# First loads, first scores and gradient sums reordered in a decode attention-and-MLP kernel with its backward pass

## The chip, the cores and the metric

The kernel runs on one core of one Trainium2 chip. The metric is the device time of one execution in microseconds (us). All timed runs quoted here are in the fast state, except e5, a single run whose state is unknown, and "time" is the median of an experiment's runs. The engines are PE (TensorE), DVE (VectorE), ACT (ScalarE), POOL (GpSimd) and SP (SyncE, which here issues the loads). "Head" is one of the 32 attention heads.

## The reference, cut to what matters

The forward pass is a gated sum of single-query attention over a cache and a small MLP; the backward pass returns gradients of all inputs.

```python
q = (x @ wq).reshape(B, Sq, H, Dh)             # x: 1x640, wq: 640x4096, 32 heads of 128
scores = einsum("bhqd,bhkd->bhqk", q, k_cache) * Dh**-0.5    # k_cache: 32 x 4096 x 128
o = einsum("bhqk,bhkd->bhqd", softmax(scores), v_cache)
a = o.reshape(B, Sq, H*Dh) @ wo                # wo: 4096x640
g = sigmoid((x * gate_w).sum(-1)); out = g*a + (1-g)*mlp(B_x)
# out, and by jax.vjp: dx, dK, dV (each 32 MB), dwq, dwo, dw1, db1, dw2, dgate_w
```

K and V are read once (2 MB per head) and dK and dV are written once (2 MB per head). With the weights and their gradients that makes 82 MB in and 82 MB out.

## The kernel before

Loads go out through SP in program order. Stores go out through GpSimd (all but the last small ones). Four K and four V buffers let the loads run ahead: K of head h+3 is issued in head h, and it needs the buffer of head h-1. The start:

```python
nc.scalar.dma_start(vec_rows[0:RC, :], x_rows)              # three first vectors, 5 rows of 256 B each, by ACT
nc.scalar.dma_start(vec_rows[RC:2 * RC, :], dy_rows)
nc.scalar.dma_start(vec_rows[2 * RC:3 * RC, :], gw_rows)
...
load_wq(0); load_wo(0); load_k(0); load_v(0); load_k(1); load_v(1); load_wo(1)    # on SP, one call per line
...  # w1, b1
load_k(2); load_v(2); load_w2(0); load_w2(1)                # w2: 96 partitions, rows of 7680 B
...  # K3 and V3 follow in head 0
```

The vectors give the gate, the gate gives the output gradient `da_bc`, and from `da_bc` and wo come four sums on DVE ("output-gradient sums"), which are broadcast as a row (`dbc`) and turned into columns (`dcol`). Small work like this sits in a list of steps. A `slot` takes from it what is ready, at most `p` PE steps and `d` DVE steps:

```python
prep_steps(0, 0)                       # qcol, doa, dob (the sums), qbc, dbc (row), dcol, qdc (columns)
for _ in range(8):
    slot(0, 9, 9)                      # all of it, ahead of head 0's scores
tk = []
for c in range(NT):
    k_chunk(0, c, tk)                  # transposes of K on PE, copied out by ACT
    if c: s_chunk(0, c - 1, tk)        # scores
...
for h in range(H):
    hh, g = h % G, h // G              # groups of four heads
    if hh == 3:
        load_wo(g + 2)                 # waits until the gradient dwo, made in the same buffer, is stored
        if g % 2 == 0:
            load_wq(g // 2 + 1)        # needs the buffer that the dx sums read
    load_k(h + 3); load_v(h + 3)
    if hh == 1 and g + 1 < NG:         # steps of the next group go to the head of the list
        rest = steps[:]; steps.clear(); prep_steps(g + 1, h); steps.extend(rest)
    period(h)                          # softmax, dV, dK, ... with three slots in it
```

## Time and profile before

| | before |
|---|---|
| time, median of 3 runs | 417.72 us (417.38 to 417.74) |
| bytes moved | 165.06 MB |
| busiest compute engine | PE and DVE, 74% each |
| DMA rate where it is full | about 420 GB/s |

165.06 MB at 422 GB/s are 391 us by themselves. These are lines of the page of the kernel before. The second is the busy share of the DMA engines in 40 equal slices, in tenths; the third is the rate in the same slices; the last is the chain of waits, by engine:

```profile
span 415.7 us, 15639 instructions
...
DMA  8999999999999999999999999999999999998980
GB/s 280 419 401 335 420 424 417 420 423 423 421 423 420 420 404 415 424 420 423 423 410 426 423 414 411 419 422 381 405 411 423 419 419 422 421 422 351 401 314 14
...
DMA 37%; DVE 30%; PE 21%; ACT 6%; issue 2%; ACTq 0%; DVEq 0%
```

The start, from the timeline of the kernel before (start, duration, engine, line, operation, count, and in brackets the idle time before and what ended it):

```profile
7.05 0.17 PE L174 MATMUL cols_ps<-ident_bf,vec_rows 15*128 15x15 bf16 x1 [7.05 <-DMA vec_rows<-in_gate_w_dram]
...
11.55 0.83 DVE L268 SCALAR_TENSOR_TENSOR junk<-wo_g,da_bc 128x640 bf16<-128x640 bf16 x1 [1.14 <-ACT da_bc L214]
...
15.25 0.61 PE L103 MATMUL d_ps<-ident_bf,do4b 128*128 128x128 bf16 x4 [2.15 <-DVE do4b L272]
...
16.66 1.87 PE L535 MATMUL tr<-ident_bf,Kn 128*128 128x128 bf16 x16
...
21.61 0.19 DVE L605 TENSOR_REDUCE m<-sA 128x1 f32<-128x32 f32 x1 [4.61 <-PE sA L543]
...
28.97 0.67 POOL L584 DMA_DIRECT2D out_dram<-dV_sb  x1 [27.58 <-DVE o_all L646]
```

PE has nothing to do until it uses the vectors at 7.05. The transposes of K stand behind the row of the output gradient (15.25) in PE's order. Head 0 proper begins with the maximum of its scores, `m`, at 21.61, and its first store is issued at 28.97.

In the middle, from the waits view of the kernel before, cut to 260 to 285 us (total, times, longest):

```profile
PE qc_ps L258 <- DMA wq_g<-in_A_wq_dram: 11.8, 1, 11.8
```

PE stands still for 11.8 us for a wq load. In this stretch the DMA runs at 424 GB/s, so by itself the wait costs nothing.

### The profile page before, as it was taken

To read this page: it belongs to the slowest core of one execution; us is meant where nothing else is said; L and a number is where in the kernel's file an instruction comes from. 1 tells how busy PE (TensorE), PEld (TensorE's weight loads), DVE (VectorE), ACT (ScalarE), POOL (GpSimd) and SP (SyncE) were. 2 spreads that over 40 slices of the span, in tenths; PEclk is the share of its full clock that TensorE was granted. 3 is DMA by queue.
4 is the path that set the end of the run, shared out by engine and by line. 5 is a ranking of instruction groups with operands and counts; after the bars stand their busy time and mean duration, and the time that the engine had idled before them with its cause. 6 is when DMAs were issued, how large, how long until landed. Compare 5 with 4: busy or idle time off the path is not lost.

```text
span 415.7 us, 15639 instructions
## 1 busy us (share of the span) xinstructions
PE 305.6 (74%) x6932; PEld 281.1 (68%) x6932; DVE 308.2 (74%) x804; ACT 174.4 (42%) x394; POOL 49.3 (12%) x92
## 2 busy tenths in 40 slices
PE   0787999888998788788877688429888788876200
PEld 0676888888987677787767687428777678876200
DVE  2348666665679999989897688528999997967850
ACT  1354444334445455354533346305553545553000
POOL 0001110111110111121111112001111111132310
PEclk9999999969999999989996899958999999998655
DMA  8999999999999999999999999999999999998980
GB/s 280 419 401 335 420 424 417 420 423 423 421 423 420 420 404 415 424 420 423 423 410 426 423 414 411 419 422 381 405 411 423 419 419 422 421 422 351 401 314 14
DMA packets 26336, 165.06 MB, mean 397 GB/s; under 512 B 2812, under 2 KB 2812, under 8 KB 10012
## 3 DMA queue, kind: packets, MB, share of 16 engines
q1 hardware_dynamic: 14116, 82.03, 48.6%
q0 software_dynamic: 12112, 82.03, 47.7%
q8 instruction: 54, 0.88, 0.8%
q14 instruction: 14, 0.11, 0.1%
q10 hardware_dynamic: 40, 0.01, 0.0%
HBM read 82.03 MB, written 82.03 MB: 395 GB/s over the span
## 4 chain that ended last, share of the span: by engine, by line
DMA 37%; DVE 30%; PE 21%; ACT 6%; issue 2%; ACTq 0%; DVEq 0%
DMA Kn<-in_A_k_cache_dram 30%; PE tr L535 7%; DVE dK_sb L557 7%; DVE dV_sb L557 6%; DMA out_dram<-dK_sb 6%; ACT tT L537 5%; DVE junk L354 4%; PE sA L601 3%; PE sA L543 3%; PE sB L654 3%; DVE junk L268 3%; PE h_ps L385 2%; DVE junk L486 2%; DMA vec_rows<-in_gate_w_dram 1%; DVE wo_g L343 1%
## 5 line engine op out<-in xcount | busy, mean ns | idle before, releaser
L537 ACT COPY tT<-tr 128x512 f32<-128x512 f32 x256 | 142.9, 587 | 153.1 <-PE tr L535 153.0
L543 PEld LDWEIGHTS <-tT 128*128 128x128 bf16 x2048 | 75.8, 98 | 37.0 <-ACT tT L537 31.6
L535 PE MATMUL tr<-ident_bf,Kn 128*128 128x128 bf16 x1024 | 79.2, 230 | 9.4 <-DMA Kn<-in_A_k_cache_dram 8.2
L557 DVE TENSOR_TENSOR dV_sb<-p_bf,qd 128x2048 bf16<-128x2048 bf16 x64 | 78.0, 1218 | 4.1 <-DMA out_dram<-dK_sb 4.1
L557 DVE TENSOR_TENSOR dK_sb<-ds_bf,qd 128x2048 bf16<-128x2048 bf16 x64 | 77.7, 1216 | 0.0
L535 PEld LDWEIGHTS <-Kn 128*128 128x128 bf16 x1024 | 66.2, 104 | 10.9 <-DMA Kn<-in_A_k_cache_dram 9.3
L535 PE MATMUL tr<-ident_bf,Vn 128*128 128x128 bf16 x1024 | 72.8, 221 | 0.2 <-DMA Vn<-in_A_v_cache_dram 0.2
L543 PE MATMUL sA<-qdc,tT 128*128 128x48 bf16 x1024 | 49.2, 188 | 23.0 <-ACT dq_all L659 16.3
L535 PEld LDWEIGHTS <-Vn 128*128 128x128 bf16 x1024 | 63.2, 100 | 1.4 <-issue 0.7
L543 PE MATMUL sB<-qdc,tT 128*128 128x48 bf16 x1024 | 46.3, 183 | 0.6 <-issue 0.6
L654 PE MATMUL sB<-ds_bf,Kn 128*128 128x48 bf16 x1024 | 32.6, 185 | 7.7 <-DVE ds_bf L643 4.8
L584 POOL DMA_DIRECT2D out_dram<-dV_sb x32 | 18.3, 571 | 169.1 <-DVE dV_sb L557 82.1
L601 PEld LDWEIGHTS <-Vn 128*128 128x128 bf16 x1024 | 30.3, 96 | 10.4 <-issue 10.3
L601 PE MATMUL sA<-e_bf,Vn 128*128 128x48 bf16 x1024 | 30.9, 183 | 7.4 <-DVE zs L621 5.4
L574 POOL DMA_DIRECT2D out_dram<-dK_sb x31 | 17.7, 570 | 153.1 <-DVE rz L623 84.6
L654 PEld LDWEIGHTS <-Kn 128*128 128x128 bf16 x1024 | 29.7, 97 | 8.3 <-issue 8.3
L605 DVE TENSOR_REDUCE m<-sA 128x1 f32<-128x32 f32 x32 | 6.1, 189 | 31.7 <-PE sA L543 31.5
L268 DVE SCALAR_TENSOR_TENSOR junk<-wo_g,da_bc 128x640 bf16<-128x640 bf16 x32 | 26.3, 821 | 2.9 <-DMA wo_g<-in_A_wo_dram 1.2
L354 DVE SCALAR_TENSOR_TENSOR junk<-wq_g,dq_bc 128x1024 bf16<-128x1024 bf16 (+1 forms) x25 | 25.1, 1004 | 0.2
L385 PE MATMUL h_ps<-cols_bf,w_sb 128*96 128x1 bf16 x90 | 18.3, 314 | 1.2 <-ACT qd L279 0.5
L641 DVE TENSOR_SCALAR_CACHE_REDUCE dj<-sB,rz 128x128 f32<-128x128 f32 x32 | 11.1, 345 | 10.8 <-PE sB L635 10.8
L385 PEld LDWEIGHTS <-w_sb 128*96 128x96 bf16 x90 | 17.6, 272 | 1.6 <-issue 0.6
(137 smaller groups left out, 277.5 us busy)
## 6 DMA issues: line engine op xcount, KB each, us to landing
Kn<-in_A_k_cache_dram SPq DMA_DIRECT2D x32, 1024.0 KB, 27.0
Vn<-in_A_v_cache_dram SPq DMA_DIRECT2D x32, 1024.0 KB, 27.8
out_dram<-dV_sb POOLq DMA_DIRECT2D x32, 1024.0 KB, 12.3
out_dram<-dK_sb POOLq DMA_DIRECT2D x31, 1024.0 KB, 12.4
wq_g<-in_A_wq_dram SPq DMA_DIRECT2D x4, 1280.0 KB, 21.8
wo_g<-in_A_wo_dram SPq DMA_DIRECT2D x8, 640.0 KB, 13.3
out_dram<-wo_g POOLq DMA_DIRECT2D x8, 640.0 KB, 11.3
out_dram<-dwq_t POOLq DMA_DIRECT2D x5, 896.0 KB, 16.2
```

Of the source, the lines that this page charges most:

```text
L268: nc.vector.scalar_tensor_tensor(junk[:, 0:D], in0=wos[g][:, i, :], scalar=1.0, in1=da_bc[:], op0=ALU.mult, op1=ALU.mult, accum_out=gp["do ...
L354: nc.vector.scalar_tensor_tensor(junk[:, c0:c1], in0=wqs[w][:, rc, c0:c1], scalar=1.0, in1=dq_bc[:, w * WG * Dh + c0:w * WG * Dh + c1], op ...
L385: nc.tensor.matmul(hps[a][:, fc:fc + 1], lhsT=w1_sb[:, rc, :].rearrange("p (q c) -> p q c", c=FCN)[:, :, fc], rhs=x_bf[:, rc:rc + 1], star ...
L535: nc.tensor.transpose(tp[:, t, :], src[:, c * 8 + t, :], ident_bf[:])
L537: nc.scalar.copy(f32v(sb[:].rearrange("p a b -> p (a b)")), f32v(tp[:].rearrange("p a b -> p (a b)")))
L543: nc.tensor.matmul(out[:, j:j + W], lhsT=tb[:, t, :], rhs=vec.to_broadcast([P, W]), start=True, stop=True)
L557: nc.vector.tensor_tensor(dst[:, a:b, :].rearrange("p j (a b) -> p j a b", b=2), col[:, a:b, :].unsqueeze(2).to_broadcast([P, n, Dh // 2, 2]),
L574: nc.gpsimd.dma_start(dKv[h], st["dK"][:])
L584: nc.gpsimd.dma_start(dVv[h], st["dV"][:])
L601: nc.tensor.matmul(O, lhsT=vts[h][:, j, :], rhs=st["e"][:, j:j + 1].to_broadcast([P, W]), start=(j == 0), stop=(j == J - 1))
L641: nc.vector.tensor_scalar(dj[:], PT, rz[:], None, ALU.mult, ALU.add, accum_out=dd[:])
L654: nc.tensor.matmul(DQ, lhsT=kts[h][:, j, :], rhs=ds[:, j, 0:1].to_broadcast([P, W]), start=(j == 0), stop=(j == J - 1))
```

## The change

The intent is to start head 0 earlier (vectors by GpSimd, K second, scores ahead of the columns) and to take the wq wait away (dwo and the dx sums, which release the wo and wq buffers, ahead of the next group's preparation; wq loaded one head earlier). Cut to its core:

```diff
-    nc.scalar.dma_start(vec_rows[0:RC, :], x_rows)            # and the two others
+    nc.gpsimd.dma_start(vec_rows[0:RC, :], x_rows)
 ...
     load_wq(0)
+    load_k(0)
     load_wo(0)
-    load_k(0)
 ...  # qdc split: qs scales the q columns early, qdc the output-gradient columns later
-        add(n("dwo"), "D", dwo, (n("aadd"),))                 # and the dx sums
+        add(n("dwo"), "D", dwo, (n("aadd"),), first=True)
 ...
-    for _ in range(8):
-        slot(0, 9, 9)
+    for _ in range(3):
+        slot(0, 1, 9)
 ...  # K transposes and scores of head 0
+    while steps:
+        slot(0, 9, 9)
 ...
+        if hh == 2 and g % 2 == 0:
+            load_wq(g // 2 + 1)                               # ahead of load_k(h + 3)
         if hh == 3:
             load_wo(g + 2)
-            if g % 2 == 0:
-                load_wq(g // 2 + 1)
 ...
-            rest = steps[:]
-            steps.clear()
+            ahead = [st for st in steps if st[5]]             # steps marked first stay in front
+            rest = [st for st in steps if not st[5]]
+            steps[:] = ahead
             prep_steps(g + 1, h)
```

More of the change, by code (lines that the diff above doesn't have):

```diff
@@ L107 @@
     vec_rows = const.tile([3 * RC, P], BF16, name="vec_rows")
-    nc.scalar.dma_start(vec_rows[0:RC, :], x_rows)
-    nc.scalar.dma_start(vec_rows[RC:2 * RC, :], dy_rows)
-    nc.scalar.dma_start(vec_rows[2 * RC:3 * RC, :], gw_rows)
+    nc.gpsimd.dma_start(vec_rows[0:RC, :], x_rows)
+    nc.gpsimd.dma_start(vec_rows[RC:2 * RC, :], dy_rows)
+    nc.gpsimd.dma_start(vec_rows[2 * RC:3 * RC, :], gw_rows)
     kts, vts, wqs, wos = {}, {}, {}, {}
@@ L227, with add @@
     steps, done = [], {}
-    def add(name, kind, fn, deps=(), head=0):
-        steps.append((name, kind, fn, tuple(deps), head))
+    def add(name, kind, fn, deps=(), head=0, first=False):
+        steps.append((name, kind, fn, tuple(deps), head, first))
     slot_no = [0]
@@ L239, in slot @@
             for st in list(steps):
-                name, k, fn, deps, head = st
+                name, k, fn, deps, head, _ = st
                 if k != kind or head > h or not room[k]:
@@ L292, in qdc, with qs @@
         def qdc():
-            gp["qdc"] = small.tile([P, 2, G], BF16, name="qdc", tag="qdc")
-            nc.vector.tensor_scalar(gp["qdc"][:, 0, :], gp["qc"][:], scale, None, ALU.mult)
-            nc.vector.tensor_scalar(gp["qdc"][:, 1, :], gp["dc"][:], scale, None, ALU.mult)
+            nc.vector.tensor_scalar(gp["dcs"][:], gp["dc"][:], scale, None, ALU.mult)
+        def qs():
+            gp["qcs"] = small.tile([P, G], BF16, name="qcs", tag="qcs")
+            gp["dcs"] = small.tile([P, G], BF16, name="dcs", tag="dcs")
+            nc.vector.tensor_scalar(gp["qcs"][:], gp["qc"][:], scale, None, ALU.mult)
         n = lambda x: f"{x}{g}"
         add(n("qcol"), "P", qcol, (), head)
+        add(n("qs"), "T", qs, (n("qcol"),), head)
         add(n("doa"), "D", do_part(0, 2), (), head)
@@ L370, in finish_steps @@
             elif g % 2 == 1:
-                add(n(f"dx{rc}_"), "D", dx(rc, 0, WG * Dh, g // 2), (n("dqb"),))
+                add(n(f"dx{rc}_"), "D", dx(rc, 0, WG * Dh, g // 2), (n("dqb"),), first=True)
     def mlp_steps():
@@ L551, in s_chunk @@
             sts[h] = {"A": sa_ps.tile([P, 512], F32, name="sA", tag="sA")}
-        products(sts[h]["A"][:, 0:J + W], ts[c], c, gp["qdc"][:, 0, h % G:h % G + 1])
+        products(sts[h]["A"][:, 0:J + W], ts[c], c, gp["qcs"][:, h % G:h % G + 1])
     def outer(dst, col, row, half):
@@ L593, in period @@
         DP, DQ, PT = B[:, 0:J + W], B[:, 128:128 + W], B[:, 256:384]
-        vec = gp["qdc"][:, 1, h % G:h % G + 1]
+        vec = gp["dcs"][:, h % G:h % G + 1]
         tv, tk = [], []
@@ L690 @@
         hh, g = h % G, h // G
+        if hh == 2 and g % 2 == 0:
+            assert g == 0 or f"dx{RC - 1}_{g - 1}" in done
+            load_wq(g // 2 + 1)
         if hh == 3:
@@ L693 @@
             load_wo(g + 2)
-            if g % 2 == 0:
-                assert g == 0 or f"dx{RC - 1}_{g - 1}" in done
-                load_wq(g // 2 + 1)
         load_k(h + 3)
```

## The prediction

> **What bounds it now.** The DMA engines. The page's slice line shows them at 9 tenths in nearly every slice, at about 420 GB/s; 165.06 MB at 422 GB/s alone is 391 us of the 415.7 us span. No compute engine is over 74% busy. 30% of the chain of waits is K loads, among them four waits of 25 to 35 us: they queue on a full DMA (the windows view shows 423 GB/s from 265 to 278 us, while PE stands still). Only DMA time that is idle or slow can be won. From the windows, in full-rate terms:
> - 0 to 7 us: start and the wq load at about 300 GB/s (3.5 us);
> - 30 to 35 us: 243 GB/s (2 us). These are w2 loads, whose 7680-byte packets take about 530 ns, a K packet 315; the first store, issued at 28.97, shows its first packet only at 34.9;
> - 245 to 255 and 280 to 300 us: about 2 us;
> - 375 to 380 us: 295 GB/s (1.5 us); then some 10 us of drain.
>
> **What the change does.** No byte goes away; it reorders.
> 1. Vectors by GpSimd. By ACT the third lands at 6.91 us (issue 1.63, 5.28 to landing), behind the 2 KB packets of wq. By GpSimd I expect 4 to 6.5 us. The Trainium skill, "DMA: Bandwidth & Descriptors", "Issuing engines are not separate DMA queues", says that all issuers share the 16 engines: no bandwidth is gained, only a place in line. If the first store's 5.9 us is a first-use cost, the vectors land no earlier, but the first store does.
> 2. K before wo. wo lands about 2.5 us later (an estimate: 1 MB at 420 GB/s), near 11 us. The output-gradient sums began at 11.55, bound by the gate chain, and become bound by wo. Steps 1 and 2 together win 0.5 to 1 us.
> 3. Scores ahead. The three slots before the scores still hold the broadcast of the output-gradient row, so K's transposes (16.66) still wait on PE for its sums (15.1). Only the columns (0.27 us on PE, plus waiting for ACT) leave the path: 0.7 us. Head 0 starts 1 to 2.5 us earlier in all, and stores begin that much earlier, beside the slow w2 loads: 0.5 to 1.5 us of DMA time.
> 4. dx and dwo ahead of the next group's sums, wq one head earlier. DVE work is the same. The dwo store goes out 3 to 5 us earlier, and SP, which waits 60 us in 5 pieces for wo's buffer (once 18 us, 225.8 to 244.4, followed by the standstill), waits less. PE's standstill may shrink by 5 us, but DMA is full there: only the dips of 245 to 300 us come back, 0.5 to 1 us.
>
> **Time.** Gains of 1 to 3.5 us, and up to 1 us lost elsewhere: 415.2 us, 80% range 412.5 to 418. 3% faster (below 409.4), 95% within, 2% slower (above 426.1).
>
> **What would show it.** Head 0's maximum of the scores at 19 to 20.5 us instead of 21.6; the last vector before 6.5; the first store issued before 28; SP's wait for wo's buffer below 45 us; the same MB and about 420 GB/s between 40 and 370; the last K load issued 1 to 4 us before 345.9.
>
> **What would make it wrong.** Vectors later than 7 us; wq, now ahead of K, holding SP until the dx sums are done, so that stores run dry; another pattern of standstills; a longer drain on the engines that finish last (26 GB/s from 404 to 411 us).

## The result, and the profile after

Ratios are the mean time of one kernel's fast runs over the mean of the other's in the same rounds, so not quite the ratio of the medians.

| | before | after |
|---|---|---|
| median | 417.73 us | 419.11 us (418.71 to 419.51) |
| ratio | | 1.0033, 95% interval 1.0016 to 1.0051 |

The change makes the kernel slower by a third of a per cent. The prediction had it faster by 2.5 us. Page of the changed kernel:

```profile
span 417.1 us, 15646 instructions
...
GB/s 277 420 402 324 421 418 419 423 423 423 420 423 420 420 420 420 422 420 422 422 416 425 419 418 425 421 353 335 395 408 423 423 423 423 421 422 390 407 311 14
...
DVE 33%; DMA 32%; PE 22%; ACT 6%; issue 4%; POOL 0%; ACTq 0%; DVEq 0%; POOLq 0%
```

The fourth slice is slower than before (324 against 335), and so are those from 270 us on (353, 335). Three slices are better by over 10 GB/s (the 15th, the 25th and the 37th). The start, from its timeline:

```profile
2.44 0.52 POOL L110 DMA_DIRECT2D vec_rows<-in_gate_w_dram  x1
...
9.10 0.17 PE L174 MATMUL cols_ps<-ident_bf,vec_rows 15*128 15x15 bf16 x1 [9.10 <-DMA vec_rows<-in_gate_w_dram]
...
17.30 0.61 PE L103 MATMUL d_ps<-ident_bf,do4b 128*128 128x128 bf16 x4 [2.15 <-DVE do4b L272]
...
17.70 1.91 PE L539 MATMUL tr<-ident_bf,Kn 128*128 128x128 bf16 x16
...
22.37 0.18 DVE L609 TENSOR_REDUCE m<-sA 128x1 f32<-128x32 f32 x1
...
29.66 0.58 POOL L588 DMA_DIRECT2D out_dram<-dV_sb  x1 [26.03 <-DVE o_all L650]
```

The vectors are used at 9.10 instead of 7.05, and everything behind them is 2.05 us late (the row of the output gradient: 17.30 instead of 15.25). The new order takes 1.3 us of that back: the maximum comes at 22.37, only 0.76 us late.

The waits of the changed kernel, cut to 250 to 275 us:

```profile
PE tr L539 <- DMA Kn<-in_A_k_cache_dram: 13.8, 1, 13.8
```

The wait for wq is gone, and a wait for K of 13.8 us has come in its place. SP's issues show why, first before and then after:

```profile
225.41 0.33 SPq L117 DMA_DIRECT2D Kn<-in_A_k_cache_dram  x1
225.80 0.47 SPq L122 DMA_DIRECT2D Vn<-in_A_v_cache_dram  x1
244.43 0.33 SPq L132 DMA_DIRECT2D wo_g<-in_A_wo_dram  x1
244.85 0.43 SPq L127 DMA_DIRECT2D wq_g<-in_A_wq_dram  x1
...
260.66 6.98 SPq L122 DMA_DIRECT2D Vn<-in_A_v_cache_dram  x1
```

```profile
221.56 0.38 SPq L127 DMA_DIRECT2D wq_g<-in_A_wq_dram  x1
225.53 7.19 SPq L117 DMA_DIRECT2D Kn<-in_A_k_cache_dram  x1
232.76 4.66 SPq L122 DMA_DIRECT2D Vn<-in_A_v_cache_dram  x1
245.38 0.33 SPq L132 DMA_DIRECT2D wo_g<-in_A_wo_dram  x1
...
251.90 3.09 SPq L122 DMA_DIRECT2D Vn<-in_A_v_cache_dram  x1
273.79 0.33 SPq L117 DMA_DIRECT2D Kn<-in_A_k_cache_dram  x1
```

The K load is issued at the same time in both (225.4 and 225.5), but in the changed kernel it stands behind 1.3 MB of wq. It is used at 268.8, 43 us later. The head that waits for it makes no stores: GpSimd issues none from 259.3 to 278.5. That alone need not cost anything. In the kernel before GpSimd issues none from 263.7 to 280.3, and the DMA stays at 424 GB/s until 280, with SP issuing loads until 267.6. In the changed kernel SP issues nothing from 255.0 to 273.8, so that loads and stores run short together:

```profile
270.00:275.00 5.00, 4.47 (x94) 4.06 (x92) 0.33 (x2) 3.25 (x6) 0.00 (x0) 0.74 0.79 308
275.00:280.00 5.00, 4.68 (x121) 4.32 (x121) 4.05 (x9) 3.46 (x7) 0.54 (x1) 1.00 0.96 395
280.00:285.00 5.00, 4.76 (x135) 4.47 (x130) 4.93 (x15) 2.21 (x6) 0.53 (x1) 1.00 0.77 298
```

These are windows of the changed kernel. Their last three columns are the granted clock, the DMA share and GB/s. The same windows of the kernel before:

```profile
270.00:275.00 5.00, 0.00 (x0) 0.00 (x0) 0.00 (x0) 0.00 (x0) 0.00 (x0) 0.50 1.01 424
275.00:280.00 5.00, 2.46 (x50) 2.18 (x51) 1.81 (x5) 0.16 (x1) 0.00 (x0) 0.50 1.01 424
280.00:285.00 5.00, 4.47 (x90) 4.27 (x88) 4.06 (x13) 2.68 (x6) 1.06 (x2) 0.72 0.95 363
```

**Where the time goes.** Both kernels move the same bytes, so I added up the trace's DMA packet records: how many bytes have landed by a given moment, and how far a kernel is behind the kernel before, in us at 420 GB/s (an own sum, from one profile each; negative is ahead):

```
                                    by 24 us  40 us   260 us  300 us  370 us  400 us
after                                 0.13    0.30   -0.49    2.53    2.47    1.09
e1  before, vectors by GpSimd         0.01    0.87    1.04    2.51    2.35    1.86
e2  before, new start order           0.01   -0.67   -0.91   -0.61   -0.59   -0.41
e4  before, new dx/dwo/wq order       0.03    0.35   -0.39    1.41    1.60    0.55
e8  two slots                        -0.08   -1.60   -1.79   -1.71   -1.74   -1.94
e9  two slots, K first                0.04   -2.12   -1.79   -1.22   -1.28   -0.73
e10 two slots, new dx/dwo/wq          0.07   -1.44   -2.12    0.14    0.28   -0.88
e11 e10 with wq behind K and V       -0.01   -2.42   -2.82   -1.95   -2.15   -2.41
e13 after, vectors by ACT             0.03   -1.09   -1.44    0.50    0.88   -0.46
e16 e11, vectors first on SP          1.01   -0.01   -0.64    0.53    0.40    0.11
```

Differences of a few tenths say little: e3 and e4 begin as the kernel before does, and are at -0.25 and 0.35 by 40 us. There are two places where kernels part: 30 to 40 us, and 260 to 300 us. A third, near 375 us, gives part of the loss back: there the kernel before falls to 295 GB/s because DVE waits for a buffer whose store has not landed, and the changed kernel has 402 GB/s in the same window and 371 in the next.

### The profile page after: what moved, and what is told of

The parts are those of the page before. It is cut to its first block, busy times and chain, and to the rows that moved or that the text cites. A ratio compares the mean times of both kernels' runs of the same rounds, so it can differ in the third digit from the quotient of the medians.

```text
span 417.1 us, 15646 instructions
## 1 busy us (share of the span) xinstructions
PE 304.5 (73%) x6932; PEld 280.9 (67%) x6932; DVE 307.7 (74%) x804; ACT 174.2 (42%) x394; POOL 51.4 (12%) x95
## 4 chain that ended last, share of the span: by engine, by line
DVE 33%; DMA 32%; PE 22%; ACT 6%; issue 4%; POOL 0%; ACTq 0%; DVEq 0%; POOLq 0%
DMA Kn<-in_A_k_cache_dram 24%; PE tr L539 8%; DVE dK_sb L561 8%; DVE dV_sb L561 7%; DMA out_dram<-dK_sb 6%; ACT tT L541 5%; DVE junk L358 4%; DVE junk L268 3%; PE sB L658 3%; PE sA L605 3%; PE sA L547 3%; DVE junk L490 2%; PE h_ps L389 2%; DMA vec_rows<-in_gate_w_dram 2%; DVE wo_g L347 1%
## 5 line engine op out<-in xcount | busy, mean ns | idle before, releaser
L539 PE MATMUL tr<-ident_bf,Kn 128*128 128x128 bf16 x1024 | 80.7, 232 | 20.7 <-DMA Kn<-in_A_k_cache_dram 19.3
L539 PEld LDWEIGHTS <-Kn 128*128 128x128 bf16 x1024 | 67.8, 105 | 22.3 <-DMA Kn<-in_A_k_cache_dram 20.3
L539 PE MATMUL tr<-ident_bf,Vn 128*128 128x128 bf16 x1024 | 71.5, 219 | 0.0
L547 PE MATMUL sA<-qcs,tT 128*128 128x48 bf16 x1024 | 48.9, 187 | 22.8 <-ACT dq_all L663 16.6
L539 PEld LDWEIGHTS <-Vn 128*128 128x128 bf16 x1024 | 62.0, 99 | 1.4 <-issue 1.0
L547 PE MATMUL sB<-dcs,tT 128*128 128x48 bf16 x1024 | 46.3, 183 | 1.3 <-issue 1.2
L605 PEld LDWEIGHTS <-Vn 128*128 128x128 bf16 x1024 | 30.3, 95 | 10.9 <-issue 10.9
L588 POOL DMA_DIRECT2D out_dram<-dV_sb x32 | 18.1, 566 | 154.9 <-DVE dV_sb L561 73.9
L658 PEld LDWEIGHTS <-Kn 128*128 128x128 bf16 x1024 | 29.3, 97 | 7.6 <-issue 7.6
L358 DVE SCALAR_TENSOR_TENSOR junk<-wq_g,dq_bc 128x1024 bf16<-128x1024 bf16 (+1 forms) x25 | 25.1, 1004 | 0.2
L629 ACT ACTIVATE p_bf<-e_bf,rz 128x64 bf16<-128x64 bf16 x32 | 11.1, 348 | 13.2 <-DVE rz L627 10.7
```

The source lines that it names most:

```text
L358: nc.vector.scalar_tensor_tensor(junk[:, c0:c1], in0=wqs[w][:, rc, c0:c1], scalar=1.0, in1=dq_bc[:, w * WG * Dh + c0:w * WG * Dh + c1], op ...
L539: nc.tensor.transpose(tp[:, t, :], src[:, c * 8 + t, :], ident_bf[:])
L547: nc.tensor.matmul(out[:, j:j + W], lhsT=tb[:, t, :], rhs=vec.to_broadcast([P, W]), start=True, stop=True)
L588: nc.gpsimd.dma_start(dVv[h], st["dV"][:])
L605: nc.tensor.matmul(O, lhsT=vts[h][:, j, :], rhs=st["e"][:, j:j + 1].to_broadcast([P, W]), start=(j == 0), stop=(j == J - 1))
L629: nc.scalar.activation(p_bf[:], e[:].unsqueeze(2).to_broadcast([P, J, 2]), ACT.Copy, scale=rz[:])
```

## The experiments

All were correct. Ratios are to the kernel before on the same chip and in the same rounds, over five rounds (six runs; e13 five), fast runs alone, except e5, which was one look.

| run | what | median us | ratio (95%) | maximum at | first store at |
|---|---|---|---|---|---|
| before | | 417.4 to 417.7 | 1 | 21.61 | 28.97 |
| after | the change | 419.11 | 1.0033 (1.0016 to 1.0051) | 22.37 | 29.66 |
| e1 | before, vectors by GpSimd | 419.54 | 1.0053 (1.0029 to 1.0078) | 23.76 | 31.37 |
| e2 | before, new start order | 416.46 | 0.9976 (0.9957 to 0.9995) | 21.03 | 28.32 |
| e3 | before, dx and dwo first | 417.32 | 0.9992 (0.9975 to 1.0009) | 22.05 | 29.40 |
| e4 | e3, wq a head earlier | 417.63 | 0.9995 (0.9976 to 1.0014) | 22.15 | 29.77 |
| e6 | before, w2 later | 418.85 | 1.0029 (1.0012 to 1.0046) | 21.81 | 29.43 |
| e7 | e6, vectors by GpSimd | 418.08 | 1.0007 (0.9991 to 1.0023) | 23.69 | 31.04 |
| e8 | e2 with two slots | 415.60 | 0.9949 (0.9932 to 0.9966) | 19.66 | 26.96 |
| e9 | e8, K first of all | 415.58 | 0.9943 (0.9930 to 0.9957) | 18.92 | 26.21 |
| e10 | e8, dx, dwo and wq as changed | 415.98 | 0.9955 (0.9939 to 0.9971) | 19.67 | 26.96 |
| e11 | e10, wq behind K and V | 415.61 | 0.9949 (0.9932 to 0.9967) | 19.11 | 26.40 |
| e12 | e11, wo behind K and V too | 418.36 | 1.0011 (0.9991 to 1.0031) | 19.03 | 26.33 |
| e13 | after, vectors by ACT | 417.33 | 0.9994 (0.9982 to 1.0006) | 21.01 | 28.31 |
| e14 | after, two slots | 417.95 | 1.0011 (0.9998 to 1.0024) | 20.89 | 28.17 |
| e15 | e11, K first of all | 416.58 | 0.9977 (0.9962 to 0.9992) | 18.81 | 26.11 |
| e16 | e11, vectors by SP ahead of wq | 416.91 | 0.9984 (0.9968 to 0.9999) | 19.78 | 28.70 |
| e17 | before, unused GpSimd loads added | 418.38 | 1.0027 (1.0010 to 1.0045) | 22.20 | 29.56 |
| e18 | before, vectors held up by ACT | 418.86 | 1.0037 (1.0022 to 1.0052) | 24.99 | 32.35 |

### Which part costs: e1 to e4

Theory "start": the late vectors cost what the change costs. Theory "wq": the load put ahead of K costs it, and a later start hides behind full DMA engines.

e1, the first line of the diff alone on the kernel before:

```diff
-    nc.scalar.dma_start(vec_rows[0:RC, :], x_rows)      # and the two others
+    nc.gpsimd.dma_start(vec_rows[0:RC, :], x_rows)
```

> The kernel before, with nothing changed but the three first vectors issued by GpSimd. The changed kernel had them at 9.1 us instead of 7.0. Theory start (the late vectors cost what the change costs): head 0's score maximum moves from 21.6 to about 23.7 us and the time rises by 1 to 2 us, to about 419. Theory wq (the wq load, put ahead of a K load, makes the stores run dry at 270 to 295 us): the same 2 us later start, but at most +0.7 us of time, because the DMA engines are full of loads until 30 us anyway.

e2, the rest of the start, vectors by ACT:

```diff
-    load_wo(0); load_k(0)
+    load_k(0); load_wo(0)
-    for _ in range(8): slot(0, 9, 9)
+    for _ in range(3): slot(0, 1, 9)                    # the rest after the scores
```

> The kernel before with K second and the scores ahead of the output-gradient columns, vectors by ACT as before, dx sums and wq loads as before. Both theories: score maximum at about 20.3 us instead of 21.6. Theory start: time falls by about 1 us. Theory wq: within 0.7 us of before.

e3, the order of dwo and dx alone; e4, with the wq load moved as well:

```diff
+        add(n("dwo"), "D", dwo, (n("aadd"),), first=True)   # e3 and e4; the dx sums too
+        if hh == 2 and g % 2 == 0: load_wq(g // 2 + 1)      # e4 alone
```

> The kernel before with dwo and the dx sums ahead of the next group's columns, but wq still loaded with wo at the last head of a group, start as before. Theory wq: no slower than before (417.2 to 418.0), no wait of PE of over 5 us for K between 250 and 290 us that before did not have; PE waits for wq there as before (11.9 us). Theory order (the new order of DVE work costs the time): +1 us or more.

> As the run before, plus the wq load one head earlier, ahead of that head's K: the whole second half of the change, start as before. Theory wq: about 419 us, slower than the run before by 1 to 2.5 us; PE waits over 10 us for a K load between 250 and 275 us, and the DMA rate falls below 350 GB/s in two 5 us windows between 270 and 295. Theory start: equal to before within 0.5 us.

Measured: the vectors by GpSimd alone cost 0.53% (2.2 us), at least as much as the whole change (the two intervals overlap). The new start order alone gains 0.24% (1.0 us). The second half does nothing that can be told from zero (-0.05%). The sum, 0.24%, is inside the interval of the change (0.16% to 0.51%). Theory start holds. My theory wq falls as the explanation of the time, although its mechanism is there: e4 waits 13.5 us for K between 250 and 275 us, e3 waits 10.8 us for wq instead, and e4 loses 1.8 us of DMA time from 260 to 300 us where e3 loses 0.7. By 400 us e4 has about 1 us less of the loss than at 370 (1.60 to 0.55), e3 0.4 us less (0.33 to -0.07).

### Why GpSimd's vectors are late: e5

```diff
+            if w == 0:                                   # zeros into wq's tile by ACT, so that its load must wait
+                for rc in range(RC):
+                    nc.scalar.copy(wqs[w][:, rc, :], hold[:].to_broadcast([P, WG * Dh]))
             nc.sync.dma_start(wqs[w][:], wq_v[...])
```

> The kernel before with the vectors by GpSimd, and the wq load (with every SP load behind it) held back some 6 us by copies of zeros into its tile, so that the DMA engines are empty while GpSimd's three loads go through. Theory queue (the vectors are late because they stand behind wq's 2 KB packets): last vector used before 5.5 us. Theory first use (GpSimd's path itself needs some 5 us at first): still 8 to 9 us.

Timeline of e5:

```profile
2.44 0.52 POOL L110 DMA_DIRECT2D vec_rows<-in_gate_w_dram  x1
...
4.31 0.10 PEld L179 LDWEIGHTS <-vec_rows 15*128 15x128 bf16 x1 [4.31 <-issue]
4.34 0.17 PE L179 MATMUL cols_ps<-ident_bf,vec_rows 15*128 15x15 bf16 x1 [4.34 <-DVE red L176]
```

With the DMA engines empty the same three loads have landed by 4.3 us. Their first packet comes 1.3 us after the first issue (1.27 to 2.6 us in the packet records). With wq in flight it comes 4.9 us after it (1.27 to 6.19), and the last at 8.0. So the queue theory holds against the first-use theory: the loads in flight make the vectors late. In which order they wait is not shown: in e9 128 packets of K go first instead of 640 of wq, and ACT's second vector shows its first packet at 4.95, as in the kernel before. ACT's vectors wait as well (the second is issued at 1.33 and shows its first packet at 4.9), but ACT issues the first at 0.74 and GpSimd at 1.27, and each of the three issues takes GpSimd 0.5 to 0.7 us, ACT 0.3 to 0.6. So 0.8 of the 2.05 us are the later issue of the third vector (2.44 against 1.63). The Trainium skill ("DMA: Bandwidth & Descriptors", "Latency and other measured facts") puts the first byte at about 0.6 us for loads issued by SP and ACT and at about 1 us for GpSimd. e5's 1.3 us by GpSimd, and 0.9 us for ACT's first load in the kernel before (0.74 to 1.68, ahead of wq's first packet at 1.86), fit that order, though both are longer; under load both figures are a small part of the 4 to 5 us.

### Why the start matters although the DMA engines are full: e6 to e9

Theory "w2": from 30 us the loads of w2 run slowly as long as no store runs beside them; a late first store makes that time longer. e6 moves the w2 loads behind the first stores, e7 does the same with GpSimd's vectors, and e8 and e9 start head 0 earlier.

```diff
-    load_w2(0); load_w2(1)                               # e6, e7: ahead of K3
+        if h in (2, 3): load_w2(h - 2)                   # e6, e7: behind K and V of heads 5 and 6
-    for _ in range(3): slot(0, 1, 9)                     # e8, e9, on e2
+    for _ in range(2): slot(0, 1, 9)                     # the row too goes behind the scores
-    load_wq(0); load_k(0); load_wo(0)                    # e9
+    load_k(0); load_wq(0); load_wo(0)
```

> The kernel before with the two w2 loads moved from ahead of K3 to heads 2 and 3, after the stores have begun. Theory w2 (a late start costs because it lengthens the time in which the slow w2 loads run alone at 240 GB/s): no window under 380 GB/s between 10 and 40 us, 1 to 2.5 us faster than before. Rival (the slow stretch belongs to the first stores or to the moment, not to w2): the slow stretch of 30 to 35 us stays, time within 0.5 us.

> The run before with the vectors by GpSimd. Theory w2: with w2 out of the way the 2 us later start costs under 1 us of time against the run before (it cost 2.1 us with w2 in place). Rival (the start is on the path to the end in itself): it costs 2 us again.

> The start of the change, vectors by ACT, with two slots instead of three ahead of head 0's scores, so that the broadcast of the output-gradient row goes behind the scores as well; wq and dx as before. Score maximum near 19 us instead of 21.0 (three slots), first store near 26.5. If the time follows the start as in the first runs (1 us for 1 to 1.5 us): 415 us.

> The two-slot start with K of head 0 loaded first of all and wq second; vectors by ACT. Theory queue: the second and third vector no longer stand behind 640 packets of wq but behind 128 of K; last vector used by 5.5 us instead of 7.0, score maximum 1 us earlier (18.5), time 0.3 to 1 us below the two-slot run. Rival (ACT's loads wait for something else): vectors at 7 us as before.

From 30 to 35 us, windows of the kernel before, of e8, of e9 and of e6, in this order (last column GB/s):

```profile
30.00:35.00 5.00, 4.53 (x125) 4.35 (x126) 4.22 (x9) 2.92 (x8) 0.53 (x1) 1.00 1.04 243
```
```profile
30.00:35.00 5.00, 4.33 (x118) 3.88 (x116) 4.89 (x15) 2.74 (x8) 0.53 (x1) 1.00 1.02 360
```
```profile
30.00:35.00 5.00, 4.33 (x115) 3.89 (x112) 4.89 (x14) 2.31 (x8) 0.53 (x1) 1.00 1.00 401
```
```profile
30.00:35.00 5.00, 4.30 (x116) 4.01 (x114) 3.75 (x9) 3.26 (x8) 0.63 (x2) 1.00 1.02 419
```

The DMA share is 1.00 to 1.04 in all four; only the rate differs. The packet records say what a w2 packet (7680 bytes) took, as a mean over the 192 packets of the two loads:

```
               first store issued   its first packet   mean w2 packet
e1                   31.4                37.5              531 ns
after                29.7                35.8              497 ns
before               29.0                34.9              477 ns
e2                   28.3                33.7              417 ns
e8                   27.0                31.1              337 ns
e9                   26.2                30.0              296 ns
```

In the kernel before, a w2 packet takes 520 to 630 ns from 31 to 35 us and 293 ns from 36 us on, when stores run beside it. K packets between them slow down as well (448 to 543 ns against 314). No run loads w2 in another form, so what makes these loads slow is open. Each step to an earlier first store shortens the slow stretch. 184 ns less for 192 packets (477 against 293), shared by 16 engines, are 2.2 us (an estimate); that is what a start could win here, and e9 wins 2.1 by 40 us.

e6 removes the slow stretch at 30 us (2.5 us ahead at 40 us), as predicted, but its time is 0.29% worse. The slow stretch came back where I had put the loads, since SP reached them when the stores had run dry. Windows of e6:

```profile
60.00:65.00 5.00, 4.24 (x90) 4.12 (x89) 1.99 (x7) 1.92 (x5) 0.53 (x1) 1.00 0.99 297
80.00:85.00 5.00, 4.20 (x117) 4.05 (x117) 4.93 (x16) 2.35 (x6) 0.42 (x1) 1.00 1.05 307
```

So e6's expected time was a miss and its mechanism was a hit. e7 tells the rest: with w2 out of the way, GpSimd's 2 us later start costs 0.06 us of DMA time by 40 us (-2.41 against -2.47), where it costs 0.87 with w2 in place. e7 is even faster than e6 as a whole, because it meets the second and third stretch differently (0.3 us behind at 90 us, e6 1.8); that part says nothing of the vectors.

e8 confirms the price of the start with the sign turned: two slots instead of three bring the maximum to 19.66 and the time to 0.51% below before. e9 has nothing more to win (its w2 packets are at 296 ns), and its time is e8's within the interval; its vectors came only 0.7 us earlier, at 6.5 us, not by 5.5 as I had expected.

### The wq load on the better start: e10 to e12

e10 is the change with vectors by ACT and two slots. e11 and e12 move loads:

```diff
-        if hh == 2 and g % 2 == 0: load_wq(g // 2 + 1)   # e11, e12
         load_k(h + 3)
         load_v(h + 3)
+        if hh == 2 and g % 2 == 0: load_wq(g // 2 + 1)
+        if hh == 3: load_wo(g + 2)                       # e12: from ahead of load_k
```

> The two-slot start with the whole second half of the change (dwo and dx first, wq one head earlier and ahead of K). If the halves add: 415.6 to 416.1 us. PE waits over 10 us for a K load near 255 to 270 us, not for wq.

> The same, but wq issued behind that head's K and V instead of ahead of them. Theory wq: the K wait of over 10 us goes away or falls under 6 us, wq is not waited for over 5 us either, the dips at 270 to 295 us shrink, 0.5 to 2 us faster than the run before. Rival (the standstill is DMA work that has to be done in any order): another load is waited for as long, same time.

> The same, and wo too issued behind K and V. Theory wq, carried on: SP's wait for wo's buffer (12 to 18 us near 245) no longer holds K back, so the standstill near 260 us shrinks further: up to 1 us faster again. Rival: same time as the run before.

e10 waits 13.4 us for K in one piece and loses 2.3 us from 260 to 300 us. e11 does not wait over 3.0 us for K and loses 0.9 there. But the medians are 415.98 and 415.61, and the intervals overlap: whether wq behind K is worth anything cannot be told from these runs. e11's waits say what came in its place:

```profile
DVE junk L268 <- DMA wo_g<-in_A_wo_dram: 11.5, 1, 11.5
...
PE qc_ps L258 <- DMA wq_g<-in_A_wq_dram: 7.9, 1, 7.9
```

e12 carried the idea on and missed: wo behind K and V came too late for the output-gradient sums, which wait 25.1 us in two pieces, and the stores run dry for it (2.7 us lost from 260 to 300 us).

### The vectors in the changed kernel, and their route: e13 to e18

e13 and e14 are the changed kernel with one line undone or altered, e15 and e16 add to e11:

```diff
-    nc.gpsimd.dma_start(vec_rows[0:RC, :], x_rows)      # e13: by nc.scalar again
-    for _ in range(3):                                   # e14: range(2)
-    load_wq(0); load_k(0)                                # e15: load_k(0); load_wq(0)
-    nc.scalar.dma_start(vec_rows[0:RC, :], x_rows)      # e16: by nc.sync, ahead of load_wq(0)
```

> The changed kernel with only the vectors given back to ACT. If the vectors' lateness is what makes the change slower: 416.5 to 417 us (419.1 minus about 2.1), first store near 28.3 us.

> The changed kernel with the vectors still by GpSimd, but two slots ahead of head 0's scores. Theory lateness (only the time at which head 0 starts counts): score maximum near 21 us, as in the kernel before, and 417 to 417.8 us. Rival (GpSimd's route costs something of its own, such as engine time for its descriptors): still 418.5 or more.

> Best parts together: vectors by ACT, K first of all loads, two slots, dwo and dx first, wq behind K and V. If the parts add: 415.0 to 415.5 us; if the start has nothing left to give (no slow stretch left at 30 to 35 us): 415.6 as the parts alone.

> Two slots and wq behind K and V, with the three vectors issued by SP ahead of every other load. Vectors used by 4 us, score maximum near 17.5 us; all other loads start about 1.4 us later. Theory DMA time (what counts is full DMA time): the 1.4 us lost at the start outweigh what the earlier start still gives: 415.6 to 416.6 us. Rival (only the start of head 0 counts, 0.8 us per us): 414.3 us.

Giving the vectors back to ACT takes the changed kernel from 1.0033 to 0.9994 (about 1.6 us; different rounds, each against before), so all of the loss hangs on that line. The packet records agree: by 40 us e13 is 1.4 us ahead of the changed kernel (-1.09 against 0.30), its w2 packets take 389 ns instead of 497, and by 400 us it is still 1.5 us ahead. The time of 417.33 us misses the expected 416.5 to 417: without the late vectors the rest of the change gains nothing that can be told from zero. e14 came out at 417.95, between the two expectations.

e15 was outside both expectations, and no better than its parts (0.9977; e9 and e11 had 0.9943 and 0.9949 in other rounds). e16 did not become the test that I meant it to be. Its vectors are used at 2.9 us, 4 us earlier than in e11, but every other load begins later, and at 24 us it is 1.0 us behind in bytes. Its sums now wait 6.5 us for wo and its scores about 1 us each for wq and K, so that the first store comes at 28.70, hardly earlier than in the kernel before. It loses about 1.4 us against e11 (0.9984 against 0.9949, in other rounds). So it shows that the vectors can't simply be put in front of everything, and it can't tell an early start from DMA time.

The last two part lateness from route. e17 adds three GpSimd loads of the vectors into a tile that nothing reads; e18 holds ACT's vectors up with copies, without GpSimd:

```diff
+    nc.gpsimd.dma_start(spare[0:RC, :], x_rows)         # e17, and the two others
+    for _ in range(11):                                  # e18, ahead of the first use of the vectors
+        nc.scalar.copy(late[:], ones_bf[:, 0:1].to_broadcast([P, 512]))
```

> The kernel before, vectors used from ACT's loads as before, with three more small loads by GpSimd of the same vectors into a tile that nothing reads. Theory lateness: head 0's score maximum near 21.6 to 22 us, time within 0.5 us of before. Rival (GpSimd's route costs time by itself): 0.8 us or more slower.

> The kernel before, vectors by ACT, with eleven copies into a spare tile on ACT ahead of the first use of the vectors, so that they are used about 2 us later with no GpSimd load at all. Theory lateness: score maximum near 23.6 us, 1 to 2.2 us slower, like the run with GpSimd's vectors; the mean w2 packet of the first two w2 loads 520 ns or more instead of 477. Rival route: time as before.

Both are slower. e18, late by 3.4 us (more than planned: the copies took 7.1 us), costs 0.37%; so lateness alone costs time, with no GpSimd load in it. It is later than e1 and costs no more, though, and its w2 packets took 508 ns, where at least 520 were expected (e1: 531). e17 costs 0.27% (1.1 us) with the vectors in time (7.13 us), which by its expectation speaks for the rival; its maximum came 0.6 us late all the same, as in e3 and e4 (22.05, 22.15), which have no such loads. By 40 us e17 is 0.3 us behind and e18 0.9; the rest of e17's loss appears after 250 us. So GpSimd's small loads may have a cost of about 1 us apart from lateness, whose mechanism no run shows. It may be no more than the standstills of 260 to 300 us falling differently: e7 has those loads too and gained on e6.

## Why the prediction was wrong, point by point

- **What bounds it** held. The bytes and the full rate are the same, and the standstills of PE cost nothing as long as the DMA stays full (424 GB/s beside the 11.8 us wait for wq). Where kernels part in bytes moved (30 to 40 and 260 to 300 us), the DMA was slow or empty.
- **The step that failed is step 1**: "By GpSimd I expect 4 to 6.5 us" for the vectors. They were used at 9.10. I had cited the skill's sentence that all issuers share the 16 engines and had drawn from it a better place in line for GpSimd's loads, which the page does not say; the trace of before had shown a GpSimd store that took 5.9 us to its first packet. I named "Vectors later than 7 us" as what would make it wrong, and it did. Alone this line costs 0.53%; the rest of the change without it is at 0.9994 (e13). So the line decides the sign, but 2.5 us would not have been reached without it either: the gain of step 4 is missing too (below).
- **Step 2** (K before wo makes the sums wait for wo) did not come up in the changed kernel, since the vectors were later still: its sums begin at 13.60, released by `da_bc`. With the vectors by ACT it does come up, as predicted: in e13 they begin at 11.69, released by wo.
- **Step 3** (0.7 us from the columns) was right: e2 has the maximum 0.6 us earlier. That three slots leave the row in front of the scores was right too, and it was the opportunity left lying: e8, with two slots, has the maximum 1.95 us ahead of the kernel before and gains 0.51%.
- **The price of the start** was right in kind: 0.5 to 1.5 us of DMA time at the w2 loads for 1 to 2.5 us. Measured by 40 us: 0.7 us for 0.6 (e2), 1.6 for 1.95 (e8), 2.1 for 2.7 (e9). The sign came from step 1.
- **Step 4** failed as well. The dwo store did not go out 3 to 5 us earlier: of the eight stores none is over 1.5 us earlier, and the fifth is 3.7 us later (287.1 against 283.5). SP's wait for wo is shorter (52.1 us in 5 pieces, longest 11.6, against 60.4 and 18.1; I had said below 45), but the longest one (18.1, now 7.9) only because it begins later, behind the V load that ends at 237.4; wo itself is issued at 245.4 instead of 244.4. That a dip of DMA time would come back for it was wrong: the standstill moved from wq to K, and the dips of 270 to 295 us grew. What I had listed under "what would make it wrong" (wq ahead of K holding SP until the dx sums are done, so that stores run dry) came true in part: SP waited 16.1 us for those sums, 10.2 ahead of the wq load at 135.2 and 5.9 ahead of that at 221.6. But the K behind the second was issued no later than before (225.53 against 225.41); it came late because wq's packets were ahead of it, and was used 43 us after its issue. In time it is worth nothing that the runs resolve (e3 against e4, e10 against e11), as about 1 us of it is given back near 375 us.
- **The sum**: +2.2 (vectors), -1.0 (start order), -0.2 (second half) make +1.0 us against +1.4 measured. Start order and second half together (e13) gain 0.06% where the parts add up to 0.29%; the intervals allow both.

What stays open: of e1's 2.2 us, 0.9 is shown at the w2 loads, and the remainder appears at 70 to 80 us and from 285 to 300 us, in stretches that e17 and e18 move as well. A cost of GpSimd's route of up to 1 us is neither shown in its mechanism nor excluded. No two of e8, e9, e10 and e11 can be told apart; they beat both kernels by 0.45 to 0.57% against before, and e8 is the simplest of them.

## What to carry to other kernels

A busy DMA is not a DMA at full rate: look for slices where the share is full and the rate is not, and ask what should run beside those transfers; an earlier first store was worth up to 2 us here, with slow loads to run beside; with these loads moved away (e6, e7) a 2 us later start cost 0.06 us of DMA time by 40 us. A small load that everything waits for came here as late as the loads already in flight made it (4.3 us with none, 9.1 with them): on this kernel moving it to another queue made it later, and issuing it before the big loads made those later. Moving a load up its queue moves everything behind it down: a wait that disappears from one tile has to be looked for at the next one in that queue.

## What the Trainium skill lacked or had wrong

- "DMA: Bandwidth & Descriptors", "Latency and other measured facts", gives a first byte of about 1 us for GpSimd and 0.6 us for SP and ACT. It has no first-byte figure beside a running load of 2 KB packets: here 4.9 us from the first issue to the first packet by GpSimd (1.3 us with the engines empty), and 3.6 us for ACT's second load.
- The same page has nothing of loads that are slow only when no store runs beside them: w2's loads (96 partitions, 7680-byte packets) took 520 to 630 ns a packet without stores and 293 ns beside them. The cause is open.
- "DMA: Bandwidth & Descriptors", "Issuing engines are not separate DMA queues", says that issuing from several engines only saves issue time. For bandwidth the runs agree. For the latency of three 1.2 KB loads, the choice of the issuing engine was worth 2 us (used at 7.05 against 9.10), of which 0.8 us are issue time.
- The same page calls engines 7 and 15 usually slower. The trace here does not name engines, so it can neither confirm nor refute that. From 405 to 410 us the kernel before moves only 26 GB/s at a DMA share of 0.06, about one engine of 16 (the page gives one engine 27 GiB/s), while nothing else is left to do.
